# Weight-block sums of the first four tile pairs taken from 32-bit weights, between the splits

## The chip, the cores and the metric

The kernel runs on one core of a Trainium2 chip. The metric is the time of one execution in microseconds on the device (us). The five engines of the core each follow an instruction list of their own: PE multiplies matrices (its weight loads are shown as PEld), DVE (VectorE) and ACT (ScalarE) do elementwise work, POOL (GpSimd) some of it too, and SP issues transfers.

## What is computed

Four batches of 768 rows go through a windowed attention with eight heads of 64, a layer norm and a two-layer feed-forward block with a residual. Cut to what matters:

```python
scores_l = scale * q @ k.T            # kept where |i - j| < 16
scores_s = scale * q @ k_sum.T + log(32)   # k_sum: maximum over blocks of 32 rows
a = softmax(concat(scores_l, scores_s))
x = a @ concat(v, v_sum)              # 4 x 768 rows of 512
xn = (x - mean) / sqrt(var + 1e-6) * g_ln
out = x + relu(xn @ w1) @ w2          # w1 512 x 2048, w2 2048 x 512
```

## The kernel before

There are 24 tiles of 128 rows (T), and they are handled in 12 pairs (g). For each pair the feed-forward block runs in eight steps, s = 8g + j. Step s multiplies the normed rows by two blocks of `w1` (`g1`, 24 matmuls of 256 columns, psum tile `h{s}`), takes the relu, and multiplies by two blocks of `w2` (`g2`). Every float32 operand is held as a float16 pair, a high part (made on ACT) and a low part (the rest, made on DVE), and each product is three matmuls: high by high, high by low, low by high.

The weights come in as pairs of 32-bit words in the `raw` tiles; `merge_w` joins them on DVE to a scaled 32-bit weight in tile `m2_f` (written `m_f` in the order's rows below). `gram` multiplies each merged block by itself on PE, and `scale_w2` reduces those sums on DVE to the scales of `w2` (the first row of that is `scales<-gram` 128x4). Only then can `split_w` make the float16 parts `w2_f`, and the part `w2_f` lies in the room of merged tile `m_{f-2}`, so a merged tile is gone once the split two places on has been written.

For the first three pairs (`PLAIN = 3`, s below 24) `g2` uses the `w2` parts as they are. From pair 3 on `g2_wide` replaces eight block products by seven with the sums of blocks that `mix_w2(i)` makes from `w2` blocks 2i and 2i+1, i from 0 to 7. In the kernel before, `mix_w2` adds high and low part of both blocks back together (two DVE adds 128x512, `wide<-w`), makes four sums of 128x256 on DVE, copies the 128x1024 result to float16 on ACT (high) and subtracts on DVE (low). All eight mixes are recorded when s reaches 24, and all splits of `w2` ahead of step 0.

Nothing is scheduled on the fly. The program's operations are first recorded by the class `Plan`, and a packed list of numbers, `ORDER`, gives the order in which they are issued: so it fixes, instruction by instruction, what each engine does after what. An instruction that has to wait holds up everything behind it on its engine. The psum tiles `h{s}` live in two banks, which they share in turn with the attention's outputs `o{T}` from tile 6 on; a tile can be written only when the relu parts of the tile that had its bank last have been read by ACT and DVE. `h23` is the first half of step 23, the last of pair 2.

Of the kernel before, what the change touches and what calls it, by code (L numbers as in the profile page):

```python
# [56 lines left out]
ORDER = (  # L57
    "c-k$P2Y6M*7KQg*5=y{Gm0m@PJd{X8dN0xxrHF-MC=pOZ1;mQwNfA&HsZymVO%RbH5Q;o{2m}l*geFCL4G_4q-hZxs`Eu_$XXec8vew#rZW+6&D="
    "KW!c2e1_n4OigN9}-0*cnMh?L1@W87X5Y82K|47rw8Y<`rdk6|yL+W|w*YZ)PNiN`+%=X2{tIzu4!s&3evu=`THGg)P51JH=|w3ffg&(p7b|uokO"
    "^UD0h7x9iGd*A!>_bwHIY)>2f~8o53Gvc`uxg*#cAs@g_1w2A8G4*JJ!fu46cwVM_H)=ss<>c*ip;Uv}z^M1N&@y2$ZZ&rCLYUi{~J=|sQEQAGKH"  # L60
# [4 lines left out]
    ";wK!Xb#cll@>!L(g!>77-{<h2RLw3gM>xdTE(=O9j)M5L>diw9JwJYuqfsO_yZBTE`B9<E!V=rljH6oWE>JLU^>;<J;b&Yimu_r-Y?Y71HG^-8n*"
    "K4l2G50QPaMn#T-A@0Mo$)cDMt+AyxpU!SE)H}&?>bmj|Cr6P3aV|X+UmCGbHB=R*d`6oPM75CyV}08^>BlHvaL}w7tgn|-__EV*@LQYf2gi|!jE"
    "I`7G|oZV_N72X&(&Pq-4vkwzgbPGjox3R2ds-cdfnd*;+D}<|~Bc%iD2P(N3$OQT84&K44Xp1xIqKusf+r8tU5NX%kp^!**D#vRjl&yIoe$-*9>T"
    "JzH$$d^2|%WJQC`GtB$NKJ*7+<Z{=N2!|DIyRCqg(1)&*p3rdXO&qRSA)hOBT~(E057`ARwq7bt6esAI`_lh~3T*aIx$5fRDp)g%^=I8i5VPBQ`E"
# [97 lines left out]
def body(ctx: ExitStack, tc, qt, qa, qe, kt, ks, va, vb, vs, g_ln, w1, w2, blocks, out):  # L166
# [838 lines left out]
    for f in range(NF):  # L1005
        split_w(f, 2)
# [87 lines left out]
```

## Time and profile before

| | |
|---|---|
| time, median of 3 runs | 595.53 us (595.12 to 595.62) |
| profiled execution: its time | 595.53 us |
| profiled execution: span | 593.7 us |
| PE busy | 581.7 us, 98% of the span |
| PEld busy | 472.1 us, 80% |
| DVE busy | 507.9 us, 86% |
| ACT busy | 426.9 us, 72% |
| POOL busy | 144.0 us, 24% |

The span runs from the first to the last instruction of the profiled execution; 1.8 us of its time lie outside the span. Busy times overlap between engines. The rows below are from five views: the page's first part (busy time by engine), the chain of waits of one engine (who held it up and for how long), windows (busy time of each engine in a stretch of the span), groups of instructions (with the mean duration of one), and the timeline (instructions in order of time).

### The profile page before, as it was taken

The numbers are of one execution on the slowest core, as the hardware profiler recorded it, in microseconds if no ns is written. First come the engines' busy times: TensorE is split into PE (matmuls) and PEld (weight loads), VectorE is DVE, ScalarE is ACT, GpSimd is POOL, SyncE is SP. The second block draws the span as 40 slices with busy tenths as digits, with TensorE's granted clock in tenths as the row PEclk, the third lists the DMA queues.
The fourth block names the chain that finished last, engine by engine and source line by source line (L and its number), as shares of the span: only waits on it lengthen the run. The fifth ranks groups of instructions, "written<-read, shape, count | busy, mean of one in ns | idle before, by whom it ended". The sixth has DMA issues, their size and how long they took to land.

```text
span 593.7 us, 16397 instructions
## 1 busy us (share of the span) xinstructions
PE 581.7 (98%) x6235; PEld 472.1 (80%) x6235; DVE 507.9 (86%) x1342; ACT 426.9 (72%) x1039; POOL 144.0 (24%) x225
## 2 busy tenths in 40 slices
PE   8989999999999999999999999999999999999997
PEld 5557678885555578888888888888888888888886
DVE  4899899999998998999988789799899889766562
ACT  4988886589787679978787865798689667553350
POOL 6342051311123012232221132423212312220101
PEclk9999999999999999999999999999999999999999
DMA  9999898644688767656685653467767623432000
GB/s 307 271 234 300 274 249 302 157 129 119 166 179 167 163 172 166 163 149 177 152 212 107 152 112 95 89 161 184 155 141 157 148 57 78 92 63 38 22 16 36
DMA packets 116261, 90.70 MB, mean 153 GB/s; under 512 B 69597, under 2 KB 100445, under 8 KB 116182
## 3 DMA queue, kind: packets, MB, share of 16 engines
q1 hardware_dynamic: 116182, 89.65, 59.9%
q8 instruction: 49, 0.80, 0.6%
q14 instruction: 30, 0.25, 0.1%
HBM read 67.05 MB, written 6.29 MB: 124 GB/s over the span
## 4 chain that ended last, share of the span: by engine, by line
PE 68%; DVE 15%; DMA 9%; ACT 4%; issue 2%; SPq 1%; POOL 0%; ACTq 0%; DVEq 0%; POOLq 0%
PE h L162 34%; PE acc_a L162 11%; PE acc_o L162 7%; PE acc_s L162 7%; DVE m L162 3%; PE s L162 3%; PE o L162 2%; DMA qs<-in_qt 2%; DVE wide L162 2%; DVE w L162 2%; DMA qs<-in_qa 1%; DMA bst<-in_vs 1%; DVE p L162 1%; PE v L162 1%; DVE h_x L162 1%
## 5 line engine op out<-in xcount | busy, mean ns | idle before, releaser
L162 PE MATMUL h<-xt,w_u 128*128 128x256 f16 x2304 | 264.5, 273 | 1.5 <-DMA xt<-x 1.4
L162 PEld LDWEIGHTS <-w_u 128*128 128x128 f16 x2304 | 224.0, 98 | 31.0 <-issue 2.4
L162 PEld LDWEIGHTS <-h_x 128*128 128x128 f16 x1752 | 170.0, 98 | 45.2
L162 DVE TENSOR_TENSOR h_x<-wide,h_x 128x896 f16<-128x896 f32 x72 | 77.9, 1088 | 14.6 <-ACT h_x L162 14.0
L162 DVE TENSOR_TENSOR wide<-wide 128x128 f32<-128x128 f32 (+1 forms) x224 | 75.2, 345 | 15.9 <-ACT wide L162 13.5
L162 ACT CAST h_x<-wide 128x896 f16<-128x896 f32 x72 | 66.8, 933 | 26.4 <-DVE wide L162 25.7
L162 POOL TENSOR_TENSOR p<-p,p 128x480 f16<-128x480 f32 x36 | 45.5, 1268 | 166.1 <-ACT p L162 130.3
L162 ACT ACTIVATE wide<-h 128x512 f32<-128x512 f32 x72 | 42.4, 591 | 38.7 <-PE h L162 24.7
L162 ACT ACTIVATE p<-p,mn,sv 128x120 f32<-128x120 f32 x144 | 68.5, 477 | 1.4
L162 PE MATMUL acc_o<-w,h_x 128*128 128x256 f16 x432 | 58.4, 273 | 0.0
L162 PE MATMUL a<-w,h_x 128*128 128x512 f16 x240 | 53.0, 379 | 0.0
L162 ACT ACTIVATE bst<-bst 128x384 f32<-128x384 f32 (+2 forms) x55 | 32.3, 587 | 18.5 <-DVE vsum L162 11.2
L162 PE MATMUL acc_a<-mix_x,h_x 128*128 128x256 f16 x324 | 45.0, 273 | 0.0
L162 POOL TENSOR_TENSOR x<-x,uv 128x512 f32<-128x512 f32 x18 | 25.3, 1418 | 77.9 <-DVE uv L162 73.6
L162 POOL TENSOR_SCALAR rs<-mv 128x1 f32<-128x1 f32 x24 | 11.8, 490 | 132.6 <-DVE mv L162 117.6
L162 PE MATMUL acc_s<-mix_x,h_x 128*128 128x256 f16 x324 | 43.9, 273 | 0.0
L162 DVE SCALAR_TENSOR_TENSOR m<-raw,m 128x512 uint32<-128x512 uint32 x64 | 42.8, 689 | 0.2
L162 PE MATMUL acc_a<-w,h_x 128*128 128x256 f16 x216 | 35.5, 273 | 0.0
L162 DVE SCALAR_TENSOR_TENSOR kl<-ksg,sv,kh 128x640 f16<-128x640 f32 x36 | 33.3, 925 | 1.9 <-ACT kh L162 1.4
L162 DVE CUSTOM_DVE_ANT_0 p<-s,mask 128x120 f32<-128x120 f32 x144 | 33.7, 272 | 1.4 <-POOL p L162 1.0
L162 ACT ACTIVATE kh<-ksg,sv 128x640 f16<-128x640 f32 x36 | 29.5, 821 | 3.6 <-DMA ksg<-in_kt 2.7
L162 ACT ACTIVATE qhl<-qs,sv 128x512 f16<-128x512 f32 x36 | 25.7, 713 | 6.1 <-DMA qs<-in_qt 4.7
(138 smaller groups left out, 888.5 us busy)
## 6 DMA issues: line engine op xcount, KB each, us to landing
raw<-in_w SPq DMA_DIRECT2D x32, 512.0 KB
ksg<-in_kt SPq DMA_DIRECT2D x36, 368.0 KB
qs<-in_qt SPq DMA_DIRECT2D x72, 128.0 KB
out_x<-x SPq DMA_DIRECT2D x24, 256.0 KB
bst<-in_ks SPq DMA_DIRECT2D x20, 192.0 KB
bst<-in_qa SPq DMA_DIRECT2D x15, 256.0 KB
bst<-in_vs SPq DMA_DIRECT2D x20, 192.0 KB
vst<-in_va SPq DMA_DIRECT2D x36, 96.0 KB
```

The source lines that it names most:

```text
L162: getattr(getattr(nc, engine), op)(*a, **k)
```

## The change

`DIRECT = 4`: the mixes 0 to 3 no longer add up float16 parts. They take the 32-bit merged weights `m2_{2i}`, `m2_{2i+1}` as they are, make the four sums of 128x256 from these, and apply the scale when the result is split: ACT's copy becomes an activation with a scale, DVE's subtraction a scalar_tensor_tensor (times the scale, less the high part). Since merged tiles are overwritten by later splits, the splits of `w2` are now recorded step by step between `g1` and `g2` of s = 0 to 7, and mix i behind step i, for i below 4. The mixes 4 to 7 stay as they were. The tiles that hold the mixes and the steps' parts have other places, the working tile `wide0` is taken earlier, and the list `ORDER` is another one from its start: all engines' instructions stand in another order. The new list is left out here and shown at three places below.

```diff
@@ -52,61 +52,62 @@
 LAG = 2
 TAIL = 3
 SOFT, WIDE = 0, 0
+DIRECT = 4
 AT = {4: 16, 5: 19, 6: 23, 7: 24, 8: 26, 9: 30, 10: 33, 11: 37, 12: 41, 13: 46, 14: 51, 15: 54, 16: 60, 17: 63, 18: 67, 19: 71, 20: 76, 21: 79, 22: 84, 23: 87}
 
 ORDER = (
...
-    "rh==uqm~;OPupb&<d0XjRULhsUtBC_V>PMPsFp=vw&STI=lpgQxcB"
...
+    "TALzCmO<`hVBPhaC@h9!dhpnD_Yz8y#O(jr<>jd#M5"
 )
 
 def block_means():
@@ -783,7 +784,7 @@
     def parts_of(s, ps):
 
         r = wide[s % 2]
-        hp = place(f"x{6 + s % 6}", f"h{s}", [P, 2, 7, P], F16)
+        hp = place(f"x{4 + s % 6}", f"h{s}", [P, 2, 7, P], F16)
         nc.scalar.activation(r[:, 4 * P :], ps.rearrange("p u t -> p (u t)"), AF.Relu)
         a, c, e, d = (r[:, (4 + i) * P : (5 + i) * P] for i in range(4))
         s1, s2, s4 = (r[:, i * P : (i + 1) * P] for i in (0, 2, 3))
@@ -797,26 +798,33 @@
         st["h", s] = hp
 
     @pl.step
-    def go_wide():
-        wide.append(work("raw", "wide0", [P, 8 * P], F32, RAW))
-        wide.append(work(f"m{NF - 2}", "wide1", [P, 8 * P]))
+    def go_wide(i):
+        wide.append(work(*(("raw", "wide0", [P, 8 * P], F32, RAW), (f"m{NF - 2}", "wide1", [P, 8 * P]))[i]))
 
     @pl.step
     def mix_w2(i):
 
-        v = place(f"y{i}" if i < YB else f"x{i - YB}", f"mix{i}", [P, 2, 4, 256], F16)
-        full = [wide[0][:, u * DM : u * DM + DM] for u in range(2)]
-        for u in range(2):
-            nc.vector.tensor_tensor(full[u], wt["w2h", 2 * i + u], wt["w2l", 2 * i + u], ALU.add)
+        v = place(("x10", "x11", "y0", "y1", "x0", "x1", "x2", "x3")[i], f"mix{i}", [P, 2, 4, 256], F16)
+        if i < DIRECT:
+            full, t = [merged[2 * i + u, 2] for u in range(2)], wide[0]
+        else:
+            full, t = [wide[0][:, u * DM : u * DM + DM] for u in range(2)], wide[1]
+            for u in range(2):
+                nc.vector.tensor_tensor(full[u], wt["w2h", 2 * i + u], wt["w2l", 2 * i + u], ALU.add)
         (b21, b22), (b11, b12) = ((x[:, :256], x[:, 256:]) for x in full)
-        t1, t3, t2, t4 = (wide[1][:, n * 256 : n * 256 + 256] for n in range(4))
+        t1, t3, t2, t4 = (t[:, n * 256 : n * 256 + 256] for n in range(4))
         nc.vector.tensor_tensor(t1, b11, b12, ALU.subtract)
         nc.vector.scalar_tensor_tensor(t3, b22, -1.0, b12, ALU.mult, ALU.subtract)
         nc.vector.tensor_tensor(t2, b22, t1, ALU.subtract)
         nc.vector.tensor_tensor(t4, b21, t2, ALU.subtract)
         hi, lo = (v[:, n].rearrange("p b t -> p (b t)") for n in range(2))
-        nc.scalar.copy(hi, wide[1][:])
-        nc.vector.tensor_tensor(lo, wide[1][:], hi, ALU.subtract)
+        if i < DIRECT:
+            sc = scales[:, 2 * i * NQ // NF : 2 * i * NQ // NF + 1]
+            nc.scalar.activation(hi, t[:], AF.Copy, scale=sc)
+            nc.vector.scalar_tensor_tensor(lo, t[:], sc, hi, ALU.mult, ALU.subtract)
+        else:
+            nc.scalar.copy(hi, t[:])
+            nc.vector.tensor_tensor(lo, t[:], hi, ALU.subtract)
         for n, l in enumerate("hl"):
             b = [wt[f"w2{l}", 2 * i + u] for u in range(2)]
             wt["mix" + l, i] = [v[:, n, 0], v[:, n, 1], v[:, n, 2], b[0][:, 256:], b[0][:, :256], v[:, n, 3], b[1][:, :256]]
@@ -1002,18 +1010,22 @@
     for f in range(NF):
         gram(f, 2)
     scale_w2()
-    for f in range(NF):
-        split_w(f, 2)
+    go_wide(0)
     go_late()
     late_masks()
-    go_wide()
 
     def feed(s):
         if s == 8 * PLAIN:
-            for i in range(NF // 2):
+            go_wide(1)
+            for i in range(DIRECT, NF // 2):
                 mix_w2(i)
         g1(s)
+        if s < NF // 2:
+            for u in range(2):
+                split_w(2 * s + u, 2)
         (g2 if s < 8 * PLAIN else g2_wide)(s)
+        if s < DIRECT:
+            mix_w2(s)
 
     done = 0
     for T in range(4, TT + LAG):
```

In number of instructions DVE loses eight adds of 128x512, and four of its subtractions of 128x1024 become scalar_tensor_tensor; on ACT four casts of 128x1024 become activations with a scale. PE, POOL and SP have the same instructions in another order.

Place 1 is on DVE, just ahead of the first row of `scale_w2`, `scales<-gram` (m_ is a merged block, h_x the low part of a step's relu, kl the low part of keys, kmax a block maximum, sv a scalar). Before:

```order
L162 SCALAR_TENSOR_TENSOR m_14_325<-raw_15_326,m_14_325 128x512
L162 TENSOR_SCALAR sv_398<-sv_398 128x1
L162 SCALAR_TENSOR_TENSOR h_x_437<-h_436,h_x_437 128x512
L162 TENSOR_REDUCE kmax_516<-bst_519 128x12
L162 SCALAR_TENSOR_TENSOR kl_348<-ksg_427,sv_398,kh_347 128x4x160
L162 TENSOR_REDUCE scales<-gram_0_327 128x4
L162 SCALAR_TENSOR_TENSOR kl_352<-ksum_373,sv_398,kh_351 128x4x24
```

And after the change:

```order
L163 SCALAR_TENSOR_TENSOR kl_333<-ksg_430,sv_401,kh_332 128x4x160
L163 SCALAR_TENSOR_TENSOR m_12_321<-raw_12_320,m_12_321 128x512
L163 SCALAR_TENSOR_TENSOR kl_337<-ksum_376,sv_401,kh_336 128x4x24
L163 SCALAR_TENSOR_TENSOR m_12_321<-raw_12_320,m_12_321 128x512
L163 SCALAR_TENSOR_TENSOR h_x_440<-h_439,h_x_440 128x512
L163 TENSOR_REDUCE kmax_516<-bst_521 128x12
L163 TENSOR_SCALAR sv_401<-sv_401 128x1
L163 SCALAR_TENSOR_TENSOR h_x_440<-h_443,h_x_440 128x512
L163 TENSOR_REDUCE scales<-gram_0_327 128x4
```

Moved: the low part of `h17`, a second `kl` of 128x4x24 and one more `kmax` now stand ahead of `scales<-gram`, and the merged block 12 is finished three rows before it.

Place 2 is on DVE, where `w2` is split (w_n is the low part of block n, mix_x the low part of a mix, wide the sums, `h_x_462` the low part of `h22`). Before:

```order
L162 SCALAR_TENSOR_TENSOR w_1_329<-m_1_299,scales,w_1_329 128x512
L162 SCALAR_TENSOR_TENSOR w_0_328<-m_0_297,scales,w_0_328 128x512
L162 TENSOR_REDUCE kmax_516<-bst_522 128x12
L162 SCALAR_TENSOR_TENSOR w_3_331<-m_3_303,scales,w_3_331 128x512
L162 SCALAR_TENSOR_TENSOR w_2_330<-m_2_301,scales,w_2_330 128x512
L162 ISA p,mn_432<-s_431,mask_424 128x120
L162 ISA mn_432 128x1
L162 ISA p,mn_432<-s_431,mask_424 128x120
L162 ISA mn_432 128x1
L162 SCALAR_TENSOR_TENSOR h_x_456<-h_455,h_x_456 128x512
L162 SCALAR_TENSOR_TENSOR w_4_332<-m_4_305,scales,w_4_332 128x512
L162 SCALAR_TENSOR_TENSOR w_5_333<-m_5_307,scales,w_5_333 128x512
```

And after the change:

```order
L163 SCALAR_TENSOR_TENSOR h_x_445<-h_457,h_x_445 128x512
L163 SCALAR_TENSOR_TENSOR mix_x_344<-wide_328,scales,mix_x_344 128x1024
L163 SCALAR_TENSOR_TENSOR w_3_347<-m_3_303,scales,w_3_347 128x512
L163 TENSOR_TENSOR wide_328<-m_3_303 128x256
L163 SCALAR_TENSOR_TENSOR wide_328<-m_2_301,m_3_303 128x256
L163 TENSOR_TENSOR wide_328<-m_2_301,wide_328 128x256
L163 SCALAR_TENSOR_TENSOR h_x_462<-h_461,h_x_462 128x512
L163 TENSOR_TENSOR wide_328<-m_2_301,wide_328 128x256
L163 SCALAR_TENSOR_TENSOR w_2_346<-m_2_301,scales,w_2_346 128x512
L163 SCALAR_TENSOR_TENSOR kl_337<-ksg_451,sv_401,kh_336 128x4x160
L163 TENSOR_REDUCE kmax_516<-bst_524 128x12
L163 SCALAR_TENSOR_TENSOR mix_x_348<-wide_328,scales,mix_x_348 128x1024
```

Moved: between the splits of blocks 3 and 2 there are now sums of mixes 0 and 1, and the splits stand further apart.

Place 3 is on PE, the first rows of `h23` and what stands ahead of it. Before, `h23` comes behind products with block 7 of `w2`:

```order
L162 LDWEIGHTS h10_x3_416
L162 MATMUL a1_0_412<-w2_7_335,h10_x3_416 128x512
L162 LDWEIGHTS w1_u14_292
L162 MATMUL h23_480<-xt_2_404,w1_u14_292 128x256
```

And after the change it comes behind `h22` and the first half of `h21`:

```order
L163 LDWEIGHTS w1_u12_288
L163 MATMUL h22_461<-xt_2_407,w1_u12_288 128x256
...
L163 MATMUL a0_0_342<-w2_1_341,h0_y0_339 128x512
L163 LDWEIGHTS w1_u10_282
L163 MATMUL h21_460<-xt_2_407,w1_u10_282 128x256
...
L163 LDWEIGHTS w1_u14_292
L163 MATMUL h23_483<-xt_2_407,w1_u14_292 128x256
```

Moved: `h23` is now ahead of the products with block 2 of `w2`; between `h22` and it PE has 18 other matmuls.

## Rows read from the trace of the kernel before

**Rows 1.** The page, part 1: busy us (share of the span) xinstructions

```profile
PE 581.7 (98%) x6235; PEld 472.1 (80%) x6235; DVE 507.9 (86%) x1342; ACT 426.9 (72%) x1039; POOL 144.0 (24%) x225
```

**Rows 2.** PE's waits: waited for, us in total, times, longest

```profile
PE gram L162 <- ACT w_u L162: 1.5, 1, 1.5
PE h L162 <- DMA xt<-x: 1.4, 3, 0.7
```

**Rows 3.** Windows: from:to, us, busy by engine, PEclk, DMA share, GB/s

```profile
100.00:120.00 20.00, 20.00 (x206) 17.74 (x205) 19.93 (x46) 11.07 (x27) 5.56 (x8) 1.00 0.68 177
120.00:148.00 28.00, 28.00 (x222) 18.97 (x220) 27.81 (x69) 25.47 (x57) 3.71 (x6) 1.00 0.43 126
...
165.00:200.00 35.00, 35.00 (x307) 17.35 (x305) 33.26 (x88) 28.47 (x73) 9.07 (x11) 1.00 0.82 174
200.00:215.00 15.00, 14.28 (x161) 10.47 (x159) 14.73 (x39) 11.49 (x26) 0.94 (x3) 1.00 0.67 180
```

**Rows 4.** DVE, groups by line and form: busy us, mean ns, idle before

```profile
L162 DVE TENSOR_TENSOR wide<-wide 128x256 f32<-128x256 f32 x80 | 33.4, 421 | 13.7 <-ACT wide L162 13.5
...
L162 DVE SCALAR_TENSOR_TENSOR w<-m,scales,w 128x512 f16<-128x512 f32 x16 | 11.3, 738 | 0.0
...
L162 DVE TENSOR_TENSOR wide<-w 128x512 f32<-128x512 f16 x16 | 10.7, 678 | 0.0
...
L162 DVE TENSOR_TENSOR mix_x<-wide,mix_x 128x1024 f16<-128x1024 f32 x6 | 7.3, 1214 | 0.0
```

**Rows 5.** ACT, groups by line and form, columns as in the group ahead

```profile
L162 ACT ACTIVATE w<-m,scales 128x512 f16<-128x512 f32 x16 | 10.9, 714 | 1.1 <-DVE w L162 1.0
...
L162 ACT CAST mix_x<-wide 128x1024 f16<-128x1024 f32 x6 | 6.2, 1037 | 0.6 <-DVE wide L162 0.6
```

**Rows 6.** DVE's timeline: start us, us, instruction, xcount

```profile
120.31 0.68 DVE L162 TENSOR_REDUCE scales<-gram 128x4 f32<-128x512 f32 x1
120.91 0.30 DVE L162 SCALAR_TENSOR_TENSOR kl<-ksum,sv,kh 128x96 f16<-128x96 f32 x1
121.14 0.15 DVE L162 TENSOR_TENSOR scales<-scales 128x4 f32<-128x4 f32 x1
...
125.66 0.73 DVE L162 SCALAR_TENSOR_TENSOR qhl<-qs,sv,qhl 64x512 f16<-64x512 f32 x1
126.32 0.87 DVE L162 SCALAR_TENSOR_TENSOR kl<-ksg,sv,kh 128x640 f16<-128x640 f32 x1
127.11 1.40 DVE L162 SCALAR_TENSOR_TENSOR w<-m,scales,w 128x512 f16<-128x512 f32 x2
128.44 0.54 DVE L162 TENSOR_REDUCE kmax<-bst 128x12 f32<-128x384 f32 x1
...
130.23 0.27 DVE L162 CUSTOM_DVE_ANT_0 p<-s,mask 128x120 f32<-128x120 f32 x1
...
130.43 0.27 DVE L162 CUSTOM_DVE_ANT_0 p<-s,mask 128x120 f32<-128x120 f32 x1
...
130.63 0.68 DVE L162 SCALAR_TENSOR_TENSOR h_x<-h,h_x 128x512 f16<-128x512 f32 x1
```

**Rows 7.** PE's timeline: start us, us, instruction, xcount

```profile
120.10 2.78 PE L162 MATMUL h<-xt,w_u 128*128 128x256 f16 x24
122.72 0.28 PE L162 MATMUL gram<-scales,ones 128*128 128x1 f32 x2
122.86 5.40 PE L162 MATMUL h<-xt,w_u 128*128 128x256 f16 x48
128.19 0.24 PE L162 MATMUL s<-kh,qhl 128*64 128x120 f16 x2
...
129.16 2.76 PE L162 MATMUL a<-w,h_y 128*128 128x512 f16 x12
131.76 2.78 PE L162 MATMUL h<-xt,w_u 128*128 128x256 f16 x24
134.38 2.75 PE L162 MATMUL a<-w,h_y 128*128 128x512 f16 x12
```

More of the change, by code (lines that the diff above doesn't have):

```diff
@@ L106 @@
-    ">QLw@vu7+Cf7ru_MmVNQMC_(sXzhyF|QV029@_3p9Ps2L_e9?Y50{3ro<7kpkKO+uHE6PDs?;z`X8iX1>Ieif(T@y3~RtzUheO}pct!3e)8b;O0v"
-    ";~w+m3SF5%~CMq4o}V9asej3urYd53c@-{;9r42;htZrRY1EL|j`x9B0N5br{axPSY%C~PZ<Lj3bfVN9g&$%TctIDy=X{3aM5*)NlwFJn(GvQUCZ"
-    "Uc$>e3T9s5vjkN;2kZay3w=<Dax;>ReZt(wG7{_;RDgfhcZ^&k5;wr)J!OyF-y<rw@Fa-EA@G_7S}HP<2OK$c|0b+D0it3VxyzGaUICs4D+l(al7"
-    "rh==uqm~;OPupb&<d0XjRULhsUtBC_V>PMPsFp=vw&STI=lpgQxcB"
+    "c-l3X2YgOv`^T^QBoPuZnn)xvtQtW{C~4IwV$?2eRYTQiYgMV$w}=`Yszw*}rmB5w)mycyHc=AP-XjQNi--}VIrsJdp2z$D<df%l&N=tE#_#%Fzx"
@@ new lines @@
+    "z~_991nLPsvp^5-Ha-T8c?F_oDdiC;3i@8!ov#^Zr8RwgyX)7HNRQ$z8pvR{h0aR4YmrcXKsfD$81JBQH8D+yXtM(;TDe)@8n*G<6oZRV3LgwXNg"
+    "`Badi;9Mz@HME5)+D@j>7qv29U{?<gfuOae4PwBH#kuf0>Eg_Dd?y^tGMtzYHH5gZ<`}8fz*K1rI)#Lg=!=$Ms$O$RIdU33`1kYMXupHOj+Mkibo"
+    "wwZjW`r5)#!4wUp*yv@)HhZ2OYI;f%_-YbuHZvG>F6Z7ljM>v(uX=;GBnB**YkY-*S3~$vBc#U?QR<BR{c}&>0H?^YiyEq^L>9Hm*lX$rG1D?6DQ"
+    "sElXtY8bdUf!BF|{BnQi;v-8D(nDp<Wjdy;_{iC(&nac(er8^4~B&hn#{l|l)Uno?ln<qthfX3EK7o$37T9@a;!_lzXzFzqFcBt!i5Kib=uqy1W6"
+    "9?NlCU)E`JQ_DPb!?>HHvA!pna?BpmzKqyv2RkS1Zmq6m%@Iad<LaQ+l^FeloyrrRbWJq>=(8rxWoHvb&R1$DyjQ)VKj<V`rFG4A&9W27cqch0nV"
@@ new lines @@
+    "O=j^bR?2_)F)ircN+T_*Ft0$aR}7aT;wd*$AoXT(XyK3z;XqOp&`xQuU%a;i~>-DiiVN*rBfsk|a5#V|9bH(o4Eb>hir#YfG#QH=FGmlkZ-W8sw}"
+    "zPwNoLI`X9%B~kVqHiv+d9a2@*oU_~YZ5?NNsUua)54JD)x*<EX8JPV``)QU`*EwV;5A3ALi{$zZO_OHQL_a0=tu&7;o@a;V(nzPtG+n{<R=qA2$"
+    "k}5pE^YOoxo-F9zjU+wqe;4kNZiv>a>3lNt@RD_t-WeK(BZ_mjU8Z`=yna1p;`<qo|a8SC|UZLk@leU(gZWyz9|=3FW+t?zAu}ha>H(-mMYrw#JQ"
+    "j3*}Yob#Oqhs7e<U?<a0?evvs<yOpKe$Z(uk`D%j5@nd@P?T+hh}P+phn`&Cbv@%8}Kb6sZH$ub<oHPVxM8!zI;)q8ff87z-%fGM&DZ0?2yf~c#h"
+    "Ce<D@B{f?2i<l5e(;4<JypEA|63y&vP@E<sZEbegMUCy0>SVf(?2!NyuJdGy-6ak6vfPnp_*IUW&X=yTNISwWW#uGZ)Yn5|)RpzJTz}R38X*OmuL"
@@ new lines @@
+    ";<^mwR=<czHb_^>nq#)Fg?ZnhUL!W;P28uYtV5a>f=n^=*a}fhZ&X<}naWH7Odeu3nN#nq%%^-&w4grkk{oH4B;D%KFI!(@(zB4>XK1adwjwGn@1"
+    "k5FDx@CPzcSZ4G^_r(}r?lTf?PbhIAxxw_c&uz@n#JTI}>zuMG>w=QTY6Jt+FEjaP4RMxBJDDkUAG|!vL_99p1^a52Cr$^;^xojiMevQ>SpwTgxZ"
+    "6nP#1-1acZ*jj3sM!sJ#pq6HED`pyIjsMXgJiSbCNko(jWeP4q{I`Y-6ob1drc)!9W8<6yt!oAie|7GWv^?b1Y=EOSoySOYfEWuCb~7`5ZvBOF4z"
+    "htL(7w~B0UF-{%HDI$2WV48B2A{Hy^u|WsbI&IMa*Yv1W%>2EXM&ypiKn%MBY#Jy$o?sMKy|xh)|tnJjx)OG<`KGVRP{H&{9ufAU<wy-l`_sR|42"
+    "vTvJJ)*C<EndKTeEUD};+YN^+_GpeB=5)9HK|u~H*8;yM?OvHC%dA)JUCc?CuA#nWw%Hi7&kl0JsJ2n$@*QW6JIL8crdQYwrX@&7wY{D7wuj8LQO"
@@ new lines @@
+    "0VX4Kpb+-A3}cm@N89TlrmY*vH!1G~|95d%YkZ+h*nhc}tRi>(lZaU1lzkzs}wArnHvkdNMQmng@8;QogsPWxSbayE&`f23RxP%(6k!)>N0x`nO$"
+    "gn%VNi#``r}GVL8(&+LH(4r`?O-F*tQJ#RL<u8uU{*q2O%%qRLUnXNWY$C$5dH6j~tg3M6u0@eZ~$=U3dgtwcSN_s=LlY!pmN9#{T#j|q|sJsYnO"
+    "Hv=PPPSVJcD?UliE@s)HJqz-mS&)*7|&ap0==k5Y&&xr-r1`=Y?yP!ZOLj8Cf3|>o0|<b+T0@Q)#)uK_)a$G+0P+M`L5MaeA;DSFm>s1jr16GwSW"
+    "pJqD}_bkED|nY6}^oJK)eM5};$TeVBX&KU&>qXTgiAg*@#EdWKT@UtrM~`9%HIf~d7{YEx!x)3sFQ5Jq(cw_Ef*EpF1JllH)h#Tu%!Ok28eJZolX"
+    "6E#Nldl_MO(+O)+6OAPhBo*jr`9d2@NxnP7+mSGId2MW#=qedU_53C+bgK;1V$@8el*6hGG8%vL<u7eSN6BE+A`=H1=CbOiIzzU}NAS!gm~ph+(o"
```

78 lines of the change are left out of this document (30 added, 48 removed).

## The prediction

> **What bounds the kernel now.** I read the page's first part, then the waits of PE, then windows, then the timelines of PE and DVE around the place that the change reorders. The page gives PE 98% of the span and DVE 86% [rows 1]; the busy share of PE is modelled, so the windows have to confirm it. They do: from 100 to 200 us PE is busy in every microsecond of the three windows shown, at a granted clock of 1.00, and a tile of 24 matmuls takes 2.62 us from its start to the next one's, 109 ns for each [rows 3, 7]. So PE issues without a gap, and its work is the same after the change. Of the span of 593.7 us, 12.0 are not PE's [rows 1]. Most lie in the first 100 us; the largest wait that the order could remove there is `gram` waiting 1.5 us for the float16 parts of `w1` [rows 2]. Later there are 0.72 us in 200 to 215 [rows 3], a part of them waits for transposed rows `xt` [rows 2]. An order that hides everything could win two or three microseconds, not more.
>
> The second engine is what can hurt. DVE is busy 19.93 of 20 us in 100 to 120 and 27.81 of 28 in 120 to 148 [rows 3], the stretch in which `w2` gets its scale and its splits. There DVE has no time of its own to make up: what is put ahead of an instruction makes it late by its full price.
>
> **The change part by part.** *Removed.* Eight adds at 0.678 us are 5.4 us of DVE [rows 4]. They were made behind the splits, where PE didn't wait, so the gain to the end is nothing by itself; the cover is PE's own unbroken work.
>
> *Added.* Four low parts as scalar_tensor_tensor of 128x1024, which the trace doesn't show: the nearest rows are the subtraction of the same size, 1.21 us, and two splits, 2 x 0.738 = 1.48 us [rows 4]. I take 1.25, near the first, since both read as many elements. On ACT the high part with a scale lies between the cast, 1.04 us, and two activations of half its size, 2 x 0.714 = 1.43 us [rows 5]; four of them cost at most 1.6 us on an engine with a quarter of its time free over the span. But in 120 to 148 ACT is busy 25.47 of 28 us [rows 3], and mixes 0 and 1 now fall there; that is a rival below. DVE as a whole gets 5.4 less 4 x 0.04 = 5.2 us less to do.
>
> *Moved.* Four mixes (four sums of 0.42 us and a low part each, about 3 us) go from behind pair 2 into the saturated stretch, between the splits; and `h23` goes on PE from behind the products with block 7 to a place ahead of those with block 2. `h23` can't start before DVE has read `h22`, whose bank it takes over. So the price of the move is how late the low part of `h22` is on DVE against PE's arrival.
>
> PE's side, from the rows of before. After the last `gram`, at 120.10, the new order puts ahead of `h23`: `h18` 2.62, the scale's matmul 0.14, `h19` and `h20` 5.33, two heads' scores 0.97, six products 1.30 (half of 2.60), `h22` 2.62, six products 1.30 and half of `h21` 1.31 [rows 7]. That is 15.59 us: PE is there at 135.7.
>
> DVE's side. An instruction starts some 0.07 us before the record of the one ahead ends: two splits take 1.33 us to the next start, 0.665 each, against 0.738 [rows 4, 6]. With that taken off: a `kl` of 128x640 0.79, `qhl` 0.66, `kmax` 0.47, a low part of h 0.61, one group of probabilities with its maximum 0.20, the small `kl` 0.23, a scalar 0.08 to 0.1, a sum of 128x256 0.35 [rows 4, 6]. The order of DVE has between `scales<-gram` and the low part of `h22`: the reduction itself 0.60, the small `kl` 0.23, eleven scalars 1.0, two `qhl` 1.32, two `kl` 1.58, seven sums of the new mixes 2.45, two `kmax` 0.93, eight groups of probabilities 1.60, three low parts of h 1.83, three splits 2.00 and the low part of mix 0 1.18; with 0.68 for the low part of `h22` it is 15.4 us. The reduction ran at 120.31 before [rows 6]. Three instructions more stand ahead of it now, a low part of h (0.61), a `kmax` (0.47) and a small `kl` (0.23): 1.3 us, and DVE was full in the 20 us before, so it starts at 121.6. The low part of `h22` is done at 137.0, PE wants the bank at 135.7: PE waits 1.3 us.
>
> Its bounds: if DVE is not late at the reduction, because the new order uses idle time of DVE earlier, it is 120.31 + 15.4 = 135.7 and the wait is nothing. If ACT's parts come late as well, by the high part of mix 0 and one of a split (1.43 + 0.71) [rows 5], it is 1.3 + 2.1 = 3.4 us. I take the 1.3. It can show in pieces, at the `gram` of block 12 (merged three rows before the reduction now), at the first products with `w2` block 0, and at `h23`; each piece makes the next smaller, and the sum is set by the last. The later splits stand further apart than before, but PE, late by then, no longer catches up with them.
>
> *Given back.* Behind the splits DVE is lighter by the four mixes and the eight adds. It was busy 33.26 of 35 us in 165 to 200 [rows 3], and the waits of 200 to 215, 0.72 us, hang on late normed rows and parts. Between nothing and 0.72; I take 0.5, since the relief (over 10 us of DVE) is much larger than the waits.
>
> The sum is made against the profiled execution, 595.53 us, which is also the median: 595.53 + 1.3 - 0.5 = 596.3 us. About 0.2%, 1.2 us, is what a measurement of this kernel can tell from no change.
>
> **The rivals.** *A, the forecast:* PE waits for DVE before or at `h23`; own range 595.2 to 597.6. *B, covered:* DVE reaches the reduction on time, out of idle time in the first 100 us; the wait is 0 to 0.2, and 595.53 + 0.1 - 0.5 = 595.1. For it: DVE had time free earlier; against it: nothing free in 100 to 120.
>
> *C, faster from the start:* the new order fills the 1.5 us at `gram` <- `w_u` and part of the wait for `xt` (1.4 in all) [rows 2]. The orders differ from the first operation on, so this can be. It decides where DVE too is ahead by that much at the reduction; then 595.53 - 1.5 - 0.5 = 593.5. Against it: PE arriving early at a full DVE waits there.
>
> *D, DVE is the real bound:* then the time falls by the work taken from it, 595.53 - 5.2 = 590.3. Against it speaks that PE has no idle time in 100 to 200 us [rows 3]; a wait of PE's cannot be removed where there is none. [...]
>
> *E, ACT and DVE late together:* ACT had 2.5 us free in 120 to 148 and gets two or three high parts of mixes of 1.04 to 1.43 us there, while every low part waits for its high part. Then each split in turn is late: 595.53 + 3.4 and some 0.8 for the last of them, less 0.5, is 599.2.
>
> **How the numbers follow.** Chances: A 0.45 (0.30 of it within 0.2%, 0.15 above), B 0.14, C 0.20, D 0.04, E 0.17. Faster by over 0.2% are C and D, 0.24; within 0.2% B and most of A, 0.44; slower E and the rest of A, 0.32. The range for 8 in 10 takes A, B and most of C and E: 593.4 to 598.9; A alone has 595.2 to 597.6.
>
> **What would show it.** In the changed kernel's trace: `scales<-gram` at 121 to 122 us (B: about 120.3, C: 119 or earlier); a wait of PE on DVE of about a microsecond between 119 and 138, in all, on `gram`, `a` or `h`; windows of PE without idle time from 140 to 200; the waits at 200 to 215 gone or smaller; mix low parts at 1.2 to 1.5 us; DVE's busy time 5 us less. Wrong would be the forecast if the first 100 us have lost or won more than a microsecond, if PE's waits behind 140 us have grown, or if PE has idle time with DVE on its chain throughout.

## The result: about 6 us slower, a percent

The changed kernel takes 602.71 us (median of 6 runs, 599.0 to 606.98), the one before 595.58 us beside it; the ratio is 1.0108, with a 95% interval of 1.0076 to 1.0141. In two later comparisons it was 1.0107 (1.0075 to 1.0139) and 1.0076 (1.0047 to 1.0105). The forecast was 596.3 us with a range of 593.4 to 598.9. The execution that was profiled took 603.83 us, with a span of 602.0; it is one of the longer ones, and two more profiles of the same kernel stand below.

The changed kernel's page, part 1, and windows of it (columns as in [rows 1] and [rows 3]):

```profile
PE 584.5 (97%) x6235; PEld 471.5 (78%) x6235; DVE 511.1 (85%) x1334; ACT 427.1 (71%) x1039; POOL 139.3 (23%) x225
```

```profile
100.00:120.00 20.00, 19.25 (x197) 16.75 (x195) 19.62 (x44) 10.19 (x26) 4.23 (x5) 1.00 0.75 177
120.00:140.00 20.00, 19.17 (x193) 15.54 (x192) 19.91 (x61) 15.92 (x37) 2.29 (x4) 1.00 0.49 139
...
200.00:215.00 15.00, 15.00 (x159) 10.26 (x158) 13.08 (x39) 10.19 (x24) 3.37 (x4) 1.00 0.63 152
420.00:440.00 20.00, 18.29 (x240) 15.63 (x238) 16.50 (x45) 16.24 (x40) 7.94 (x7) 1.00 0.81 188
500.00:520.00 20.00, 18.58 (x220) 16.35 (x218) 15.69 (x42) 14.13 (x37) 5.39 (x6) 1.00 0.34 69
```

PE has idle time now where it had none, or next to none (0.23 us in 420 to 440): 0.75 us in 100 to 120, 0.83 in 120 to 140 (20 less the busy time), 1.7 in 420 to 440, 1.4 in 500 to 520. The idle 0.72 us of 200 to 215 [rows 3] are gone in this execution. DVE's busy time did not fall by the 5 us that were named as a sign: it is 511.1 us here and 507.2 and 507.5 in two later profiles, against 507.9. Part of that is that the same instructions run longer behind step 24: the low parts of values (36 instructions `v<-vst,sv,v`) have a mean of 766 ns in the kernel before, and in the new head with the old tail below, and 792 to 819 in the changed one; why stays open.

Four low parts of mixes now use the scale, and their price is inside its bounds; groups of DVE and of ACT (columns as in [rows 4, 5]):

```profile
L163 DVE SCALAR_TENSOR_TENSOR mix_x<-wide,scales,mix_x 128x1024 f16<-128x1024 f32 x2 | 2.6, 1278 | 0.0
...
L163 ACT ACTIVATE mix_x<-wide,scales 128x1024 f16<-128x1024 f32 x2 | 2.3, 1137 | 0.0
```

In the stretch that the forecast was made for DVE took as long as it was worked out. DVE's timeline of the changed kernel, with the first row of the scale, the low part of mix 0 and the low part of `h22`:

```profile
123.34 0.68 DVE L163 TENSOR_REDUCE scales<-gram 128x4 f32<-128x512 f32 x1
...
135.21 1.28 DVE L163 SCALAR_TENSOR_TENSOR mix_x<-wide,scales,mix_x 128x1024 f16<-128x1024 f32 x1
...
138.09 0.68 DVE L163 SCALAR_TENSOR_TENSOR h_x<-h,h_x 128x512 f16<-128x512 f32 x1
```

From the reduction's start at 123.34 to the end of the low part of `h22` at 138.77 it is 15.43 us; the forecast's sum was 15.4. PE's rows with a wait in that stretch, and its first product of pair 3, which ends the head of the kernel:

```profile
115.24 2.78 PE L163 MATMUL h<-xt,w_u 128*128 128x256 f16 x24 [0.75 <-DVE h_x L163]
...
121.52 1.09 PE L163 MATMUL gram<-m 128*128 128x128 bf16 x16 [0.42 <-DVE m L163]
...
125.39 0.38 PE L163 MATMUL gram<-scales,ones 128*128 128x1 f32 x2 [0.16 <-DVE scales L163]
...
128.42 4.10 PE L163 MATMUL h<-xt,w_u 128*128 128x256 f16 x36 [0.25 <-DVE h_x L163]
...
217.37 0.83 PE L163 MATMUL acc_s<-mix_x,h_x 128*128 128x256 f16 x6
```

PE waits in pieces: at `h` for a low part (0.75) ahead of the scale, then at `gram` for a merged block (0.42), at the scale (0.16) and at `h` for a low part (0.25). Of the three places that the forecast named only the `gram` shows a wait; at the first products with `w2` block 0 and at `h23` there is none. PE comes to its first product of pair 3 (step 24) at 217.37; before, that was at 214.86.

### The profile page after: what moved, and what is told of

It reads as the page before. It is cut to its first block, busy times and chain, and to the rows that moved or that the text cites. A ratio compares the mean times of both kernels' runs of the same rounds, so it can differ in the third digit from the quotient of the medians.

```text
span 602.0 us, 16405 instructions
## 1 busy us (share of the span) xinstructions
PE 584.5 (97%) x6235; PEld 471.5 (78%) x6235; DVE 511.1 (85%) x1334; ACT 427.1 (71%) x1039; POOL 139.3 (23%) x225
## 4 chain that ended last, share of the span: by engine, by line
PE 68%; DVE 14%; DMA 8%; ACT 5%; issue 2%; POOL 2%; SPq 0%; ACTq 0%; DVEq 0%; POOLq 0%
PE h L163 29%; PE a L163 10%; PE acc_a L163 9%; PE acc_s L163 6%; PE acc_o L163 6%; DVE m L163 3%; PE s L163 3%; PE o L163 2%; DMA bst<-in_ks 2%; DMA raw<-in_w 2%; DVE h_x L163 2%; DVE p L163 1%; DVE kl L163 1%; DVE x L163 1%; DVE wide L163 1%
## 5 line engine op out<-in xcount | busy, mean ns | idle before, releaser
L163 DVE TENSOR_TENSOR h_x<-wide,h_x 128x896 f16<-128x896 f32 x72 | 79.6, 1109 | 17.7 <-ACT h_x L163 17.3
L163 POOL TENSOR_TENSOR p<-p,p 128x480 f16<-128x480 f32 x36 | 43.9, 1219 | 167.5 <-ACT p L163 157.8
L163 POOL TENSOR_SCALAR rs<-mv 128x1 f32<-128x1 f32 x24 | 15.1, 629 | 126.5 <-DVE mv L163 109.8
L163 DVE CUSTOM_DVE_ANT_0 p<-s,mask 128x120 f32<-128x120 f32 x144 | 35.0, 272 | 3.8 <-PE s L163 3.6
L163 DVE SCALAR_TENSOR_TENSOR v<-vst,sv,v 128x512 f16<-128x512 f32 x36 | 29.3, 819 | 4.1 <-ACT v L163 4.1
```

Source lines behind the costliest of these rows:

```text
L163: getattr(getattr(nc, engine), op)(*a, **k)
```

## Experiments: where the time is lost

Both orders list the same operations but for the eight adds (and the form of the four high and four low parts), and at the first matmul of step 24 (some 215 us) they have done nearly the same ones. So the lists can be cut there and joined crosswise. I call what lies ahead of the cut the head, what lies behind it the tail. What each run is, as a diff of the order:

```diff
 head_new_tail_old (changed code)
-ORDER: new list
+ORDER: new list up to g1(24), then what is left as in the old list
 head_old_tail_new (code of before)
-ORDER: old list
+ORDER: old list up to g1(24), then what is left as in the new list
 start_old_middle_new_tail_old (changed code)
+ORDER: old list up to g1(16), new list up to g1(24), old list
 new_to_step_56, new_to_step_72 (changed code)
+ORDER: new list up to g1(56) or g1(72), then the old list
```

**The changed kernel again.**

> The changed kernel once more, nothing edited. Order theory (the new list behind pair 2 lets PE run into DVE, ACT and late transfers): 599 to 607 us again, and PE's waits behind 240 us stand at the same instructions as in the first profile (h on xt near 430, s on kl near 502, h on ACT's wide near 251 and 279). Chance theory (transfers happened to land late in that execution): the time is within 0.3% of before, or the waits stand elsewhere.

It took 600.52 us (ratio 1.0107). The waits near 430 and 500 are there again, those near 251 and 279 are not.

> The changed kernel, beside its own parts on one chip. By the two profiles so far, PE's steady losses against before are 2.4 us in 100 to 140 us and 2.1 to 3.6 us behind 400 us, and -1.6 to +0.9 in the first 100 us: a ratio of 1.008 to 1.012, waits at h on xt (about 425) and s on kl (about 500) again.

602.17 us, 1.0076, just under the band.

**Head new, tail old.**

> The changed kernel's code and its order up to the first matmul of step 24, then the remaining operations in the order of the kernel before. Order theory (5.8 of the 8.3 us are lost behind step 24 by the new list there): 595.6 + 0.9 (first 100 us) + 2.4 (100 to 140) - 0.7 = 598.2 us, 597.2 to 599.5. Rival (the head leaves attention or transfers late, and the loss behind is its consequence): 601 us or more.

596.94 us, ratio 1.0029 (1.0015 to 1.0043), just under the band.

> New order up to step 24, old behind. If the late stretch is worth 2 us or more, it is 2 to 4 us below the changed kernel of the same chip, ratio to before 1.002 to 1.006. Rival (the first result was that chip's luck): within 1 us of the changed kernel.

598.34 us, ratio 1.0051 (1.0029 to 1.0073), 3.8 us below the changed kernel beside it.

**Head old, tail new.**

> The code of the kernel before with its own order up to the first matmul of step 24, mixes made from float16 parts as before, then the remaining operations in the new order. Order theory: 595.6 + 5.8 = 601.4 us, 599.5 to 603. Rival (the loss is the head's consequence): 595 to 597 us.

598.63 us, ratio 1.0053 (1.0034 to 1.0072): slower than before with the old kernel's whole head, though less than the band said.

**Cuts in the tail.**

> The changed kernel with its own order up to the first matmul of step 56 (about 380 us), the order of before from there. Order theory, spread: the waits at 250 to 300 stay and those at 430 and 500 go: 596.9 + 0.6 to 1.9 = 597.5 to 598.8 us. Rival (all of the tail's loss is in the late third, at 430 and 500): 596.9 us as with the old tail. Other rival (the loss is before step 56): 600 us or more.

602.67 us, 1.0095 (1.0071 to 1.0119).

> New order up to step 56, old behind. Late theory (the tail's loss is at about 430 and 500 us): as the run with the old tail, within 0.2%. Rival (what is lost lies between steps 24 and 56, or comes of the list as a whole): as the changed kernel.

601.29 us, 1.0086 (1.0058 to 1.0114): as slow as the changed kernel, so the times alone gave the rival right.

> New order up to step 72 (about 460 us), old behind: it has the wait at 430 and not the one at 500. Late theory: between the run with step 56 and the changed kernel, 1 to 2 us below the changed kernel. Rival: as the changed kernel.

600.42 us, 1.0057 (1.0035 to 1.0079): 1.8 us below the changed kernel beside it, as the late theory had it, but the run with step 56 isn't lower still.

**Only the middle new.**

> The changed kernel's code; the order of before up to the first matmul of step 16 (about 106 us), the new order from there to the first matmul of step 24, then the order of before again. So only the stretch in which the mixes 0 to 3 are made is new. Order theory, with the forecast's term for this stretch (1.3 to 2.4 us of waits of PE on DVE, 0.5 given back): 596.4 to 597.5 us. Rival (the change pays for itself once the other parts of the list are undone): 594.5 to 595.5 us.

599.35 us, 1.0065 (1.0044 to 1.0087), worse than with the whole new head beside it (1.0029) and outside both bands. In its profile PE waits 1.5 us for low parts of h (two waits, the longest 1.2), where it has 0.5 behind the new start; the joint at step 16 may cost something by itself, so this run tells nothing on either theory.

The times of one kernel spread over 5 to 8 us here, those of the kernel before over 3 to 5, and a ladder of fifths of a percent can't be read from them. The traces can: the start of the first product of pair 3 is the length of the head, from there to the start of PE's last matmul is the tail. Its row in four of the runs, in this order: before, changed_again, head_new_tail_old, head_old_tail_new:

```profile
214.86 0.83 PE L162 MATMUL acc_s<-mix_y,h_x 128*128 128x256 f16 x6
```

```profile
215.14 0.83 PE L163 MATMUL acc_s<-mix_x,h_x 128*128 128x256 f16 x6
```

```profile
214.41 0.83 PE L110 MATMUL acc_s<-mix_x,h_x 128*128 128x256 f16 x6
```

```profile
214.52 0.83 PE L109 MATMUL acc_s<-mix_y,h_x 128*128 128x256 f16 x6
```

The lengths, one profile each, in us:

| list in the head | list in the tail | heads | tails |
|---|---|---|---|
| old (before; adds left out) | old | 214.86, 214.55 | 374.81, 376.65 |
| new (two runs) | old | 214.41, 214.96 | 375.75, 375.59 |
| old | new | 214.52 | 378.00 |
| new (changed kernel, three profiles) | new | 217.37, 215.14, 217.15 | 380.58, 377.02, 379.23 |
| new (two runs) | new to step 56 | 220.23, 216.17 | 376.88, 377.99 |
| new | new to step 72 | 216.28 | 376.08 |
| middle alone new | old | 217.35 | 376.27 |
| old order with one, two and four direct mixes (below) | old | 218.04, 220.55, 226.16 | 376.23, 376.08, 376.48 |
| new, edited twice (below) | old | 217.72, 216.36 | 375.68, 375.62 |

The new heads of the first six rows have a mean of 216.5, 1.9 us more than the old list's 214.6 but with a wide spread. The old tails of the first two rows have a mean of 375.7, the four new ones of 378.7: 3.0 us more. The tails are the firmer of the two: all ten old ones lie below 376.7 and the four new ones above 377.0. By these profiles head and tail lose 5 of the 5.6 to 7.1 us between the medians. The first of the two runs with a cut at step 56 was slow by its head (220.23), as the trace shows and the time can't.

**The clock of the first 20 us.** The spread of the heads has a cause that the record shows in part. Windows of the changed kernel's first and third profile and of new_to_step_56, and the same four matmuls in the first and the last of these:

```profile
0.00:20.00 20.00, 15.93 (x124) 10.81 (x125) 11.20 (x47) 10.49 (x41) 12.71 (x64) 1.00 0.94 312
```

```profile
0.00:20.00 20.00, 15.77 (x121) 10.46 (x121) 9.60 (x40) 9.34 (x37) 11.72 (x60) 0.91 0.95 314
```

```profile
0.00:20.00 20.00, 17.06 (x101) 11.44 (x102) 9.69 (x40) 9.35 (x37) 11.84 (x60) 0.85 0.93 311
```

```profile
15.30 1.98 PE L163 MATMUL v<-spare_x,blk 128*120 128x512 f32 x4
```

```profile
16.14 3.77 PE L110 MATMUL v<-spare_x,blk 128*120 128x512 f32 x4
```

The granted clock is 0.72 from 14 to 20 us in the second and 0.50 from 16 to 20 us in the third, and what is lost there is still missing at the first matmul of `h`: it starts at 41.53 to 41.57 us in every new head whose clock stayed at 1.00, at 43.18 in the second and at 44.74 in the third. The mean granted clock is on record for every execution, and the times go with it. Of the changed kernel's 18 executions the eight at 0.999 or more have a mean of 600.1 us, the four at 0.994 one of 603.8. All 91 executions with the old head (the kernel before, the eight adds left out, the old head with the new tail) lie at 0.996 or more; of the 78 with the new head (the changed kernel, the old tail, the cuts at 56 and 72, the two edited heads) 16 lie at 0.993 or 0.994. So a lower clock, and with it a longer time, comes more often with the new head.

At 0.999 or more alone, where the clock can take little part, the mean times are: before 595.9 us (59 executions), new head and old tail 597.2 (17), old head and new tail 598.3 (8), both new 600.1 (8). The head then costs 1.2 us, the tail 2.4, both together 4.2; the heads of the profiles without a low clock at the start agree, 215.7 in the mean of six against 214.7 of two, 1.0 us. Some 1.2 us of the loss over all executions (601.5 in the mean against 596.1, 5.4) is left for the clock.

What recurs in the tail is in all four profiles with the new list there. PE's waits behind 400 us in changed_again, and the one at `s` behind the old head, in head_old_tail_new:

```profile
PE h L163 <- DMA xt<-x: 1.1, 1, 1.1
PE s L163 <- DVE kl L163: 0.9, 1, 0.9
```

```profile
497.81 0.24 PE L109 MATMUL s<-kl,qhl 128*64 128x120 f16 x2 [0.94 <-DVE kl L109]
```

`s` waits 0.94 us for `kl` in each of the four, `h` waits 1.0 to 1.4 us for the transposed rows `xt` near 425 to 430. Behind the new head with the old tail, neither is there; all that the view of PE's waits lists from 215 us on (head_new_tail_old_again):

```profile
PE acc_a L110 <- DVE h_x L110: 0.2, 1, 0.2
PE s L110 <- DVE qhl L110: 0.2, 1, 0.2
```

The wait at `s` can be followed back along the chain that ended last, in changed_again:

```profile
488.29 1.15 POOL rs L163
...
489.54 4.05 DMA vst<-in_vb
...
493.69 0.73 ACT v L163
...
494.45 0.04 DVE v L163
...
496.65 0.76 DVE kl L163
...
497.45 0.56 PE s L163 x14
```

SP issues a load of values (`vst<-in_vb`) only at 489.54. The chain puts that down to POOL's `rs`, done at 489.44; SP's own timeline has a transposing transfer just ahead of the load, which it issued right after POOL's `p` was done at 488.20:

```profile
488.23 1.25 SPq L163 DMA_TRANSPOSE pt<-p  x1
```

Its issue ends at 489.48, so which of the two held the load isn't told; in the other three profiles with the new tail both end within 0.1 us of each other too. The load lands four microseconds later, ACT's `v` and DVE's `v` wait for it, and `kl` and then `s` on PE stand behind `v` on DVE. In that order of the instructions one late load holds two engines and then PE; no run moves the load alone. With the cut at step 72 this wait is gone and the one at `xt` is left, 0.9 us (from PE's waits).

The two waits are about 2 of the tail's 3 us. Where the rest lies is not settled: with the cut at step 56 neither wait is there, yet the tails are 1.2 and 2.3 us longer than the old ones' mean, and with the cut at step 72, which has one of the waits, only 0.4. One profile each can't put these in order, and the medians, 601.29 and 600.42 us beside one another, can't either.

## Experiments: what the change itself costs

**Eight adds left out, nothing moved.**

```diff
         full = [wide[0][:, u * DM : u * DM + DM] for u in range(2)]
-        for u in range(2):
+        if i < 4:
+            full = [wt["w2h", 2 * i + u] for u in range(2)]
+        for u in range(2 * (i >= 4)):
             nc.vector.tensor_tensor(full[u], wt["w2h", 2 * i + u], wt["w2l", 2 * i + u], ALU.add)
```

> The kernel before in its own order with the eight adds of mixes 0 to 3 left out (the sums are made from the high parts alone, so the mixes lack the low parts' share): DVE has 5.4 us less to do and nothing is moved. Forecast's theory (PE is the bound, the adds are covered): 594.5 to 595.2 us against 595.0, within 0.2%. Rival D (DVE is the bound): 595.0 - 5.4 = 589.6 us, 588 to 592.

596.04 us beside 597.17 for before, ratio 0.9986 (0.9969 to 1.0002). Its page, part 1, and a window:

```profile
PE 583.6 (98%) x6235; PEld 472.2 (79%) x6235; DVE 504.0 (85%) x1334; ACT 426.8 (72%) x1039; POOL 145.3 (24%) x225
```

```profile
120.00:148.00 28.00, 28.00 (x227) 19.27 (x226) 27.45 (x68) 25.77 (x58) 3.71 (x6) 1.00 0.44 128
```

DVE is 3.9 us less busy, PE is busy 28.00 of 28 us as before [rows 3]. The adds were covered; by the interval they were worth 1.9 us at most.

**The changed code in the old order.** Only what the code forces is moved: the four sums of a mix ahead of the splits that overwrite its blocks, its parts ahead of the next mix's sums.

```diff
 DVE, old order, from the first splits on (bare_change_old_order: mixes 0 to 3)
 w2_1 low, w2_0 low
+wide<-m 128x256 x4 (mix 0)
 w2_3 low, w2_2 low
+mix_x low (mix 0)
+wide<-m 128x256 x4 (mix 1)
 w2_4 low, w2_5 low
...
-wide<-w 128x512 x2 and the rest of mixes 0 to 3, behind the splits
```

> The changed kernel's code in the order of before; only what the code forces is moved: the sums and parts of mixes 0 to 3 stand between the splits that overwrite their blocks. Forecast's theory (what is put into the full stretch of DVE is late by its price, less the lead that the splits had): up to the split of block 8 four times four sums (5.6 us) and three low parts (3.6 us) are added, the lead was some 4 to 7 us, so PE waits 2 to 5 us, and 597 to 600 us come out. Rival (the relief behind pays for it): 594.5 to 595.5 us.

610.93 us, ratio 1.0247 (1.0223 to 1.0272): 14.8 us, three times the upper end. PE's rows with the two long waits, and windows around them (the last columns are the granted clock, DMA share and GB/s):

```profile
134.74 5.15 PE L110 MATMUL h<-xt,w_u 128*128 128x256 f16 x24 [4.67 <-DVE h_x L110]
```

```profile
159.91 0.24 PE L110 MATMUL s<-kh,qhl 128*64 128x120 f16 x2 [5.05 <-DVE mn L110]
```

```profile
134.70:139.80 5.10, 5.06 (x25) 3.62 (x26) 4.76 (x9) 2.10 (x3) 0.00 (x0) 0.52 0.00 0
139.80:154.80 15.00, 15.00 (x95) 7.92 (x93) 12.65 (x30) 12.13 (x28) 0.00 (x0) 1.00 0.24 70
...
159.90:170.00 10.10, 10.09 (x53) 4.63 (x53) 6.28 (x17) 7.24 (x21) 1.74 (x3) 0.83 0.73 198
```

Two waits for DVE of 4.7 and 5.1 us; and behind each the 24 matmuls or the products run at a granted clock of 0.52 and 0.83, `h` taking 5.15 us instead of 2.78 [rows 7].

**One mix and two mixes** (`DIRECT = 1`, `DIRECT = 2`, the same way).

```diff
-DIRECT = 4
+DIRECT = 1
```

> The changed code with DIRECT = 1 in the order of before: only mix 0 is made from the 32-bit weights, its four sums (1.4 us) ahead of the splits of blocks 2 and 3, its parts (1.2 us on DVE) ahead of those of 4 and 5. Lead theory (DVE may be late by what the next user's lead is; the low part of h20 had 0.5 us, the splits 4 us): PE waits 1 to 2 us in 120 to 150, time +0.5 to +2 us. Rival (each mix costs its share of the 14.6 us of four): +3.6 us. Other rival (covered): within 0.5 us.

> The same with DIRECT = 2: 5.2 us of DVE work put between the splits. Lead theory: PE waits 3 to 5 us, time +3 to +5 us. Share rival: +7.3 us. Covered: within 0.5 us.

600.34 us, ratio 1.0079 (1.0057 to 1.0101), and 603.32 us, 1.0121 (1.0095 to 1.0147), beside 595.81 for before: +4.7 and +7.2 by the ratios. One mix costs more than its share of 3.6, two cost just theirs, 7.3; the lead theory (0.5 to 2, 3 to 5) has neither. The timelines of one_direct_old_order, DVE's, ACT's and PE's, tell why (in brackets the idle time ahead of the row and who ended it):

```profile
127.70 0.41 DVE L110 TENSOR_TENSOR wide<-m 128x256 f32<-128x256 f32 x1
128.04 0.41 DVE L110 SCALAR_TENSOR_TENSOR wide<-m,m 128x256 f32<-128x256 f32 x1
128.37 0.87 DVE L110 TENSOR_TENSOR wide<-m,wide 128x256 f32<-128x256 f32 x2
...
132.12 1.28 DVE L110 SCALAR_TENSOR_TENSOR mix_x<-wide,scales,mix_x 128x1024 f16<-128x1024 f32 x1 [0.89 <-ACT mix_x L110]
...
133.52 0.69 DVE L110 SCALAR_TENSOR_TENSOR h_x<-h,h_x 128x512 f16<-128x512 f32 x1
```

```profile
128.54 1.52 ACT L110 ACTIVATE w<-m,scales 128x512 f16<-128x512 f32 x2 [1.40 <-DVE wide L110]
...
130.95 1.14 ACT L110 ACTIVATE mix_x<-wide,scales 128x1024 f16<-128x1024 f32 x1
```

```profile
134.26 4.22 PE L110 MATMUL h<-xt,w_u 128*128 128x256 f16 x24 [3.38 <-DVE h_x L110]
```

```profile
130.90:134.20 3.30, 0.00 (x0) 0.00 (x0) 2.41 (x8) 2.41 (x4) 0.65 (x3) 1.00 0.33 99
134.20:138.30 4.10, 4.04 (x25) 3.08 (x26) 4.10 (x12) 3.40 (x7) 0.00 (x0) 0.65 0.00 0
```

`h22` needs the low part of `h20`, which ends at 134.2. Ahead of it on DVE stand the four sums (127.70 to 129.16, 1.46), 0.89 idle, in which DVE waits for ACT's high part of the mix, and the low part (1.20): 3.55 us, where the low part had a lead of 0.45 (its end at 131.31 against 131.76 [rows 6, 7]). The difference, 3.1, is close to the wait of 3.38. ACT in its turn stood 1.40 us, since it can't write the split over block 1 before DVE has read it. Then PE, idle for 3.3 us, goes on at a granted clock of 0.65, and `h` takes 4.22 us: 1.44 us more. 3.38 and 1.44 are 4.8, near the measured 4.7, but that match is partly luck. At step 24 this execution (218.04) is only 3.2 us behind the kernel before (214.86): it came to `h22` 0.9 us earlier (134.26 less 3.38, against 131.76), and 0.7 us of idle time in 200 to 220 are gone. Its tail, 376.2, is inside the range of the old ones.

## Experiments: the lateness in the new head

```diff
 head_new_scale_early: DVE, new head, old tail
+merge of block 12
 kl, kl, h16 low
-merge of block 12
+scales<-gram 128x4
 kmax, sv, h17 low
-scales<-gram 128x4
 head_new_chain_early: DVE, new head, old tail
-kmax, h17 low
 scales<-gram, two products, scales<-scales 128x1
+kmax, h17 low
```

> As the run with the new head and the old tail (596.9 us), but block 12 of w2 is merged four rows earlier on DVE, and the reduction scales<-gram stands ahead of the three instructions (kmax, sv, low part of h17) that the change put before it. Forecast's theory (the lateness of the reduction is what the head costs): 1.0 to 1.9 us less, 595.0 to 595.9 us. Rival (the head's loss lies in its first 100 us or in the sums between the splits): 596.4 to 597.4 us, no difference.

601.53 us, ratio 1.0077 (1.0047 to 1.0107), in another comparison than the plain new head. Not less but more.

> New head, old tail, and in the head kmax and the low part of h17 stand behind the scale's second reduction (scales<-scales of 128x1), so the whole chain runs 1.1 us earlier. Forecast's theory (these rows ahead of the chain are what is late): PE's losses in 100 to 140 fall from 2.4 to about 1.3 us, the time by about a microsecond against the run with the new head (ratio 1.002 instead of 1.004). Rival (DVE is full, so what is taken from one place is late at the next, and the last wait sets the sum): 2 us or more are left in 100 to 140, the time is the same.

601.38 us, ratio 1.0096 (1.0065 to 1.0127). PE's row with the largest wait in that stretch, in the first and in the second:

```profile
125.54 0.38 PE L110 MATMUL gram<-scales,ones 128*128 128x1 f32 x2 [1.45 <-DVE scales L110]
```

```profile
127.90 4.11 PE L110 MATMUL h<-xt,w_u 128*128 128x256 f16 x36 [1.48 <-DVE h_x L110]
```

In the first, the wait at `gram` for a merged block is gone, and the scale's matmul waits 1.45 us, for the last reduction of the chain stayed where it was: that edit didn't test what it was made for. In the second the scale doesn't wait, and `h` waits 1.48 us for a low part. That is not the low part of `h17` that was put behind, but the next one; DVE's rows of head_new_chain_early:

```profile
122.93 0.68 DVE L110 SCALAR_TENSOR_TENSOR h_x<-h,h_x 128x512 f16<-128x512 f32 x1
...
126.05 0.55 DVE L110 TENSOR_REDUCE kmax<-bst 128x12 f32<-128x384 f32 x1 [1.13 <-DMA bst<-in_ks]
...
127.16 0.68 DVE L110 SCALAR_TENSOR_TENSOR h_x<-h,h_x 128x512 f16<-128x512 f32 x1
```

The first of these is the moved one, done at 123.61. The one that PE waits for starts at 127.16, behind the work that was moved there (1.1 us) and behind a `kmax` that stood 1.13 us for its load. PE is idle for 2.8 us in 100 to 140, the 2 us or more of the rival; but the rival's reason, that DVE is full and what is taken from one place is late at the next, isn't shown by it, since DVE itself was idle for 1.6 us of 120 to 140 in this execution. So neither edit settles whether the lateness of the scale is what the head costs. The times of both are above the head they started from; how much of that is the edit stays open, as the times of one kernel spread as far.

## Why the prediction was wrong, point by point

- **PE is the bound, removed adds are worth nothing:** right. Without them and nothing else moved, 0.9986 (0.9969 to 1.0002). Rival D, by which the time would fall by 5.2 us, is out.
- **Moved, PE waits 1.3 us for DVE:** right in mechanism and near in size, wrong in the places. DVE's 15.4 us from the reduction to `h22` were 15.43; PE's idle time in 100 to 140 is 1.58 us in the changed kernel, 0.83 of it between 119 and 138, where about a microsecond was forecast. The reduction was later than forecast (123.34, not 121.6), but so was PE: its `h` behind the last `gram` starts at 122.45, not at 120.10. So DVE came out 0.7 us late against PE, not 1.3, and PE had spent that before `h23`. For the head the forecast's net was 1.3 less 0.5, 0.8 us; measured are 1.0 to 1.2 at full clock.
- **Given back, 0.5 us:** right in size: of the idle 0.72 us of 200 to 215 the three profiles of the changed kernel have 0, 0.27 and 0.49 left, so 0.5 was given back in the mean. But the step that failed stands here. The sum ends with this term, and so takes the rest of the program behind step 24 for unchanged. The new list reorders that too, and there it loses 2.4 to 3 us: each time the same waits of 0.94 at `s` and 1.0 to 1.4 at `h`, behind a load and a transpose that land late, and smaller ones. The forecast compared the orders near `scale_w2` alone, and no term or rival priced the loss of an order behind it. "Its work is the same" was true of PE and no argument on its waits. Of the signs that the forecast named for being wrong, this is the one that came: PE's waits behind 140 us have grown.
- **A term that isn't there, the clock:** the forecast took the granted clock of 1.00 for given in the new list as well. In some executions it is lower in the first 20 us (0.91 and 0.85 in two profiles), more often with the new head; about 1.2 us of the mean is put down to it, an estimate from the difference of the mean times, 5.4 us over all executions less 4.2 at 0.999 or more.
- **Rival C** had the orders' difference everywhere, but as a gain in the first 100 us. None is seen: no new head comes to step 24 more than 0.5 us ahead of the old one's 214.86, and one list's head varies from 214.4 to 220.2 between executions.
- **Rival E** (ACT and DVE late together, 599.2 us) would have been the nearest in time, but not for its reason: in 120 to 140 PE is idle for 0.83 us in the changed kernel, not for the 3.4 and more that E needs. The chain of E is what the old order shows, with idle times of 1.40 us on ACT and 0.89 on DVE for one mix. The range, up to 598.9, left E's own 599.2 outside, though it was said to hold most of E.
- **What the change costs in the old order** was priced too low before that run: 14.8 us instead of the 2 to 5 expected. Left out were the new waits between ACT and DVE (a mix's high part waits for the sums, its low part for the high part, a split for the sums), and the slower clock behind the two long waits (0.52 behind 4.7 us, 0.83 behind 5.1). The new list hides all of that but 1 to 2 us; so the list, not the removed adds, is most of what was changed.

Not settled is why the clock is lower at the start of some executions and not of others, and why more often with the new head: `after` and changed_third have nearly the same waits of PE ahead of it (1.30 and 1.46, then 0.50 and 0.4 us between 7 and 13 us). What is left of the spread without it, 597.8 to 603.8 us in the changed kernel at 0.999 or more, is open too.

## What to carry to other kernels

Work that is covered earns nothing when it is removed (0.9986 without the eight adds), and can cost more than its price where it is put (14.8 us for four mixes of about 3 us in the old order): look for the stretch in which the second engine is full, and for the lead of each of its results there, before you move work into it. When an order is made anew, compare it to the end; a list that is worked over to make room in one place can lose as much in places that the change never touched (2.4 to 3 us in the tail here). And where times spread by a percent, cut the program at a fixed instruction and compare the lengths of the pieces in the traces, and compare executions of the same mean clock with each other.

## What the runs showed of the hardware

Behind three waits of 3.4 to 5.1 us PE's granted clock was lower. After 3.3 us in which PE did nothing (130.9 to 134.2 in one_direct_old_order) the clock of the next 4.1 us was 0.65, and 24 matmuls that took 2.78 us in the kernel before [rows 7] took 4.22. After 4.7 us idle (bare_change_old_order) it was 0.52 from 134.7 to 139.8, and 1.00 again from 139.8 to 154.8, in which PE was busy throughout; after the 5.1 us idle behind that it was 0.83 from 159.9 to 170. In the changed kernel's first profile, with waits of 0.75 us and less in 100 to 140, it stayed at 1.00 there.

In the first 20 us the changed list had a mean clock of 1.00 in one execution and of 0.91 in another, with nearly the same waits of PE ahead (1.30 and 1.46 us the longest between 7 and 13 us). Four matmuls of `v` that took 1.98 us in the first of these took 3.77 us in new_to_step_56, where the clock was 0.50 from 16 to 20 us; that execution came to step 24 at 220.23, the other of the same list at 216.17.
